# Planned costs of the Fourier sets, and the order of the products in K's table sets

## The chip, the cores and the metric

One core of a Trainium2 chip runs the kernel. The metric is device time in microseconds (us): the median of several executions. The core's engines each work through a list of instructions in order: TensorE (PE) multiplies matrices into PSUM; VectorE (DVE), ScalarE (ACT) and GpSimd (POOL) do elementwise work; SyncE (SP), POOL and ACT start DMA transfers.

## The reference

The output mixes two layers of one input, u (2048 tokens by 512 channels), with a gate per token. a is a state space layer: a kernel K(d, l) of 2048 taps for each channel, convolved with u by FFTs of length 4096, plus a skip term. b is a gated linear unit on x.

```python
def _A_ref(u, log_A_real, A_imag, C_real, C_imag, log_dt, D_skip):
    dt = jnp.exp(log_dt)
    A = -jnp.exp(log_A_real) + 1j * A_imag
    C = (C_real + 1j * C_imag) * dt[:, None]
    P = jnp.exp((A * dt[:, None])[:, :, None] * pos[None, None, :])
    K = 2.0 * jnp.einsum("dn,dnl->dl", C, P).real
    Kf, Uf = jnp.fft.rfft(K, 2 * L), jnp.fft.rfft(u_t, 2 * L)
    y = jnp.fft.irfft(Uf * Kf[None, :, :], 2 * L)[:, :, :L]
    return y.transpose(0, 2, 1) + u * D_skip[None, None, :]

def _B_ref(x, w_gate, w_up, w_down):
    h = jnp.einsum("bsd,df->bsf", x, w_gate) * jnp.einsum("bsd,df->bsf", x, w_up)
    return jnp.einsum("bsf,fd->bsd", h, w_down)

g = _sigmoid((x * gate_w).sum(-1, keepdims=True))
return g * a + (1 - g) * b
```

## The kernel before, in words

The GLU (b) fills PE from beginning to end. Its 14 tiles of hidden features are taken in four groups, and within a group four chunks of 512 tokens are gone through. Each float32 factor is split into a high and a low part, so that one product becomes three matmuls of 128 by 128 by 512 ("whi", "wlo", "hh", "hl", "dhi", "dlo" are such parts). `product` (line 580) issues three for the gate or up projection into `pg` or `pu`, `down` (line 623) three for the down projection into `y`. Between them ACT and DVE make h = gate times up and its two parts, `hh` and `hl`.

The state space layer (a) is put between the GLU's matmuls as *sets*: each set is one task of PE, a run of small float32 matmuls that use the array split into tiles. Each float32 product stands in the trace as two weight loads and two matmuls. The sets, all writing PSUM banks called `k`:

- `u_part`, `first` (line 731 on): the first transform of u, 8 sets, tiles of 32 rows by 64 columns.
- `k_block`, `kgen` (lines 1081 and 1084): the **table set**, 16 of them, one for each block of 32 channels. DVE and ACT build two tables of powers, x and v, for the block; PE multiplies them, for each channel d one product with the real parts (c = 0) and one with the imaginary parts (c = 1), which accumulate in one place. A product has 128 rows, 32 columns of weights and 64 moving columns, and goes to the column tile d % 4 of the array, which is also the quarter of the bank's partitions that it writes. After the set ACT and DVE fold the bank `pk` into `kt`.
- `k_first` (line 1112): K's first transform, 8 sets on four tiles of 32 rows by 128 columns.
- `m_second` (line 1197): second transforms of u and K, 16 sets, tiles of 32 by 32.
- `m_inverse` (line 1254): after the product of the spectra, the first inverse transform, 8 sets, tiles of 32 rows by 64 columns.
- `m_last` (line 1304): the last inverse transform, 5 sets, tiles of 64 by 32; one for two groups of rows or for one.

The order of the work is not written by hand. Every piece is a task, given to `add` with its engine, a cost in us, its operands, a rank and the tiles that it holds. `Work.run` (line 301) is a list scheduler: it keeps a clock for each engine, works out when each task could start (operands ready, buffer free, engine free), and takes the task with the earliest start; rank decides between equals. Sets that carry `many` are kept at least 6 us (4 us in the last parts) from the end of the one before. The list that comes out is each engine's order of instructions, for the DMA queues too. On the chip only that order counts: an instruction starts when its operands are there and its engine has done what stands before it. The costs given to `add` therefore never cost time themselves; they only shape the order.

All instructions pass through one helper, so every row of the profile names line 124; rows are told apart by the names of their tiles.

Of the kernel before, what the change touches and what calls it, by code (L numbers as in the profile page):

```python
# [20 lines left out]
KT = D // P  # L21
# [343 lines left out]
def gated_mix_kernel(  # L365
# [365 lines left out]
    def u_part(t):  # L731
        ut = inp([P, 4, D])
        rs = slice(4 * t, 4 * t + 4)
        add("sp", 0.42, lambda: sp.dma_start(ut.t, uv[:, rs, :]), w=[ut], dma=1024, after=6.0 + (U_STEP + 1.0) * t)

        def score_of(j):
            r = 4 * t + j
            pr = new("mid", "y", [P, D], bufs=2)
            add(
                "dve", 0.73,  # L740
                lambda: dve.scalar_tensor_tensor(
                    pr.t, ut.t[:, j, :], 1.0, gw.t, op0=ALU.mult, op1=ALU.mult, accum_out=gate[:, r : r + 1]
                ),
                r=[ut, gw], w=[pr, (m_gate, ("s", t))], rank=0,
            )

        for j in range(4):
            score_of(j)
        ones = [new("mid", "y", [P, 2, D], bufs=2) for _ in range(2)]
        ops = (ALU.add, ALU.subtract)  # L750
        for y, op in zip(ones, ops):
            add(
                "dve", 1.22,
                lambda y=y, op=op: dve.tensor_tensor(out=y.t, in0=ut.t[:, :2], in1=ut.t[:, 2:], op=op), r=[ut], w=[y],
            )
        for s, op in enumerate(ops):
            for d, y in enumerate(ones):
                add(
                    "dve", 0.69,
                    lambda d=d, s=s, y=y, op=op: dve.tensor_tensor(  # L760
                        out=ut.t[:, 2 * s + d], in0=y.t[:, 0], in1=y.t[:, 1], op=op
                    ),
                    r=[y], w=[(ut, 2 * s + d)],
                )

        def first(s):
            banks, st = [bank() for _ in range(4)], new("mid", "ev", [P, KT, 4, P], bufs=2)

            def fn():
                for p in range(2):  # L770
                    col, src = 64 * (p + s), 2 * s + (p + s) % 2
                    for tq in range(4):
                        lanes = slice(32 * tq, 32 * tq + 32)
                        pe.matmul(
                            banks[tq].t[64 * p : 64 * p + 64], w1_t.t[lanes, col : col + 64], ut.t[lanes, src],
                            start=True, stop=True, tile_position=(32 * tq, 64 * p),
                        )

            add("pe", 1.3, fn, r=[(ut, 2 * s), (ut, 2 * s + 1), w1_t], w=banks, rank=1, hold=[st])
            for tq in range(4):  # L780
                add(
                    "act", 0.59,
                    lambda tq=tq: act.copy(st.t[:, :, tq], banks[tq].t.rearrange("p (f d) -> p f d", f=KT)),
                    r=[banks[tq]], w=[(st, tq)],
                )
            n0 = 16 * s + 4 * t
            for q in range(KT):
                add(
                    "pool", 0.95,
                    lambda q=q: pool_q.dma_start(  # L790
                        su_d[q, :, n0 : n0 + 4, :], st.t[:, q],
                    ),
                    r=[st], w=[(m_su, (q, n0))], dma=256,
                )

        for s in range(2):
            first(s)
        sc, ga = (m_gate, ("s", t)), (m_gate, t)
        add("act", 1.5, lambda: act.activation(gate[:, rs], gate[:, rs], AF.Tanh, scale=0.5), r=[sc], w=[sc], rank=0)

        def gates():
            dve.tensor_scalar(ngate[:, rs], gate[:, rs], -0.5, 0.5, op0=ALU.mult, op1=ALU.add)
            dve.tensor_scalar(gate[:, rs], gate[:, rs], 0.5, 0.5, op0=ALU.mult, op1=ALU.add)

        add("dve", 0.4, gates, r=[sc], w=[ga, sc], rank=0)
# [272 lines left out]
    def apart_of(q):  # L1078
        return work.LESS if q >= KT - 2 else work.APART

    def k_block(b, x, v):
        pk = bank()

        def kgen():
            pv = pk.t.rearrange("p (g j) -> p g j", j=64)
            for d in range(TB):
                ch, g = d % 4, d // 4
                for c in range(2):
                    pe.matmul(
                        pv[32 * ch : 32 * ch + 32, g, :], x.t[:, c, d, :], v.t[:, c, d, :], start=c == 0, stop=c == 1,  # L1090
                        tile_position=(0, 32 * ch),
                    )

        if b % 4 == 0:
            kts["now"] = new("tab", "kt", [P, 2, 2, 32, 16])
        kt, g0 = kts["now"], b % 4 * 8
        add("pe", 2.15, kgen, r=[x, v], w=[pk], rank=0, hold=[kt], many=work.APART, slack=5.0 if b < 16 else 0.0)
        pv = lambda a: pk.t.rearrange("p (g a b k) -> p g a b k", a=2, b=2, k=16)[:, :, a]
        side = lambda h: kt.t[:, h, :, g0 : g0 + 8].rearrange("p b g k -> p g b k")
        add("act", 0.37, lambda: act.copy(side(1), pv(0)[:, :, :, ::-1]), r=[pk], w=[(kt, (1, b % 4))])  # L1100
        for h, op in enumerate((ALU.add, ALU.subtract)):
            add(
                "dve", 0.42, lambda h=h, op=op: dve.tensor_tensor(out=side(h), in0=pv(1), in1=side(1), op=op),
                r=[pk, (kt, (1, b % 4))], w=[(kt, (h, b % 4))], rank=0,
            )
        if b % 4 == 3:
            k_first(b // 4, kt)
# [4 lines left out]
    def k_first(q, kt):  # L1112

        tt(
            0.24, lambda: kt.t[:, :, 0, :, 0], lambda: kt.t[:, :, 0, :, 0],
            lambda: skip[:, q].unsqueeze(1).broadcast_to([P, 2, 32]), ALU.add, [m_skip], [kt],
        )
        for h in range(2):
            banks = [bank() for _ in range(4)]
            if q < KT - 1:  # L1120
                st = new("mid", "ev", [P, 16, 4, 32], bufs=2)
                sts = [(0, 16, st)]
            else:
                shape = [P, 8, 4, 32]
                pair = [new("tab", n, shape) for n in ("ri", "e")] if h else [stage(shape) for _ in range(2)]
                sts = [(0, 8, pair[0]), (8, 8, pair[1])]

            def fn(h=h, banks=banks):
                for b in range(2):
                    for c in range(4):  # L1130
                        lanes = slice(32 * c, 32 * c + 32)
                        pe.matmul(
                            banks[c].t, w1k_t[lanes, b, 64 * h : 64 * h + P],
                            kt.t[lanes, h, b].rearrange("p g k -> p (g k)"),
                            start=b == 0, stop=b == 1, tile_position=(32 * c, 0),
                        )

            add("pe", 1.95, fn, r=[kt, m_w1k], w=banks, rank=-1, hold=[st for _, _, st in sts], many=apart_of(q))
            for n0, n, st in sts:
                for c in range(4):  # L1140
                    ns = slice(n0, n0 + n)
                    evict(
                        q, c, 0.2 + 0.025 * n, lambda c=c, st=st: st.t[:, :, c, :],
                        lambda c=c, banks=banks, ns=ns: banks[c].t.rearrange("p (g n) -> p n g", n=16)[:, ns],
                        [banks[c]], [(st, c)],
                    )
                n0 += 16 * h
                add(
                    "sp", 0.42,
                    lambda n0=n0, n=n, st=st: sp.dma_start(  # L1150
                        sk_d[q, :, n0 : n0 + n, :], st.t.rearrange("p n c g -> p n (c g)"),
                    ),
                    r=[st], w=[(m_sk, (q, m)) for m in range(n0, n0 + n, 8)], dma=64 * n,
                )
# [42 lines left out]
    def m_second(q, T, ins, w):  # L1197
# [13 lines left out]
                to = banks[r].t[32 * c : 32 * c + 32].rearrange("l (p d) -> l p d", p=2)[:, p]  # L1211
                pe.matmul(to, w.t[lanes, m], src[lanes, c, p], start=True, stop=True, tile_position=(32 * r, 32 * c))

        add("pe", 1.05, fn, r=[*parts, w], w=banks, rank=1, hold=[to])
        for r in range(4):
            h, e = divmod(r, 2)
            evict(
# [36 lines left out]
    def m_inverse(q, T0, ys, ws):  # L1254
# [18 lines left out]
                                    ys[t].t[lanes, k, e, cs], start=k == 0, stop=k == 1, tile_position=(32 * j, 64 * e),  # L1273
                                )

        add("pe", 2.13, fn, r=[*ys, *ws], w=[*banks, (m_turn, (q, T0))], rank=1, hold=sts, many=apart_of(q), slack=0.0 if q < KT - 1 else 0.0)
        for j in range(4):
            st, m = sts[j // 2], j % 2
            evict(
# [24 lines left out]
    def m_last(q, gs):  # L1304
# [14 lines left out]
        def fn():  # L1319
# [8 lines left out]
                        )  # L1328

        add(  # L1330
            "pe", 0.2 + 0.86 * len(gs), fn, r=[*src, m_w4, *([(m_turn, (KT - 1, 2))] if q == KT - 2 else [])], w=[b for bs in banks for b in bs], rank=1,
            hold=[to for _, to, _, _ in pieces],
        )
        cs = slice(P * q, P * q + P)
# [155 lines left out]
```

## Time and profile before

| what | value |
|---|---|
| median of 3 runs | 588.23 us (587.84 to 588.41) |
| span of the profiled execution, first to last instruction | 586.6 us |
| outside the span (median less span) | 1.6 us |
| DMA traffic | 136.28 MB, mean 232 GB/s |

The page gives no device time of the profiled execution itself beside its span, so the median of the runs stands for it; the 1.6 us are before the first and behind the last instruction. In rows of the timeline the first number is the start and the second the time until the last of the merged instructions ends; matmuls are pipelined, so one of them starts long before the one before it has ended, and it is the distance between starts that counts. In a row of groups, "k<-v,x 128*32 128x64 f32 x2048" is a tile written from two others, the rows and columns of the array in use, the moving operand, and the count. "PEld" is the loading of weights.

### The profile page before, as it was taken

Reading aid. Unit: us, or ns where it says so; the run is one execution under the profiler, and the core shown is the slowest. Engines: PE = TensorE matmul, PEld = TensorE weight load, DVE = VectorE, ACT = ScalarE, POOL = GpSimd, SP = SyncE. Lnnn points to the kernel's source line nnn. Section 1 sums busy time; section 2 is a strip of 40 time slices with the busy share of each in tenths; the row PEclk is TensorE's granted clock in tenths of the full one; section 3 lists DMA queues with packets and bytes.
Section 4 is the critical chain, followed back from the end, with each engine's and each line's share of the span. In section 5 each row is a group of like instructions: output and inputs, shape, how many; then the busy total and the mean of one; then the engine's idle time right before and its main releaser. Section 6 shows DMA issues by size and latency. Waiting matters only on the chain.

```text
span 586.6 us, 14827 instructions
## 1 busy us (share of the span) xinstructions
PE 576.4 (98%) x5996; PEld 433.9 (74%) x5996; DVE 511.3 (87%) x812; ACT 399.0 (68%) x891; POOL 113.4 (19%) x159
## 2 busy tenths in 40 slices
PE   8999999999989999999999999999999999999997
PEld 5777777877876777887777778777878787677775
DVE  6998999999999999999799999995999982367664
ACT  5468888898578589876968764899696523443351
POOL 0002222311102231310412200421321104011011
PEclk9999999999999999999999999999999999999999
DMA  8999969997647698998697859899958349899976
GB/s 276 383 369 357 374 241 319 289 257 212 125 154 181 194 272 205 228 245 297 135 257 249 183 180 304 158 187 276 221 136 212 65 143 230 290 270 253 283 159 125
DMA packets 71687, 136.28 MB, mean 232 GB/s; under 512 B 6852, under 2 KB 35780, under 8 KB 69188
## 3 DMA queue, kind: packets, MB, share of 16 engines
q1 hardware_dynamic: 47668, 87.10, 43.0%
q0 software_dynamic: 23392, 47.98, 39.5%
q8 instruction: 47, 0.77, 0.6%
q10 hardware_dynamic: 560, 0.26, 0.2%
q14 instruction: 20, 0.16, 0.1%
HBM read 80.27 MB, written 55.05 MB: 231 GB/s over the span
## 4 chain that ended last, share of the span: by engine, by line
PE 83%; DVE 6%; ACT 4%; DMA 4%; issue 1%; SPq 0%; DVEq 0%; ACTq 0%
PE pg L124 23%; PE pu L124 23%; PE y L124 22%; PE k L124 16%; DVE v L124 1%; DMA pb<-par_d 1%; DMA xs_d<-xs 1%; DVE x L124 1%; DMA y<-in_xT 1%; DMA xs<-xs_d 1%; ACT acc L124 1%; DVE t L124 1%; ACT ev L124 1%; ACT xs L124 1%; ACT e L124 1%
## 5 line engine op out<-in xcount | busy, mean ns | idle before, releaser
L124 PE MATMUL pg<-xs,whi 128*128 128x512 f32 x448 | 138.9, 391 | 1.0 <-DVE xs L124 0.6
L124 PE MATMUL pu<-xs,whi 128*128 128x512 f32 x448 | 138.3, 390 | 0.0
L124 PEld LDWEIGHTS pg<-xs,whi 128*128 128x128 f32 x448 | 84.2, 188 | 20.2 <-ACT whi L124 2.0
L124 PEld LDWEIGHTS pu<-xs,whi 128*128 128x128 f32 x448 | 84.2, 188 | 16.9
L124 PE MATMUL y<-dhi,hl 128*128 128x512 f32 x224 | 90.3, 403 | 2.9 <-DVE hl L124 2.4
L124 PE MATMUL pu<-xs,wlo 128*128 128x512 f32 x224 | 90.1, 402 | 0.0
L124 PE MATMUL pg<-xs,wlo 128*128 128x512 f32 x224 | 89.4, 399 | 0.4 <-ACT h L124 0.4
L124 PE MATMUL y<-dlo,hh 128*128 128x512 f32 x224 | 87.5, 391 | 0.0
L124 PE MATMUL y<-dhi,hh 128*128 128x512 f32 x224 | 87.3, 390 | 0.0
L124 POOL DMA_DIRECT2D out<-acc x44 | 40.2, 968 | 180.4 <-ACT acc L124 173.0
L124 ACT COPY ev<-k 128x512 f32<-128x512 f32 x112 | 58.8, 596 | 14.5 <-PE k L124 14.4
L124 ACT CAST hh<-h 128x512 fp32r<-128x512 f32 x56 | 34.6, 618 | 45.7 <-DVE h L124 45.5
L124 PEld LDWEIGHTS y<-dhi,hl 128*128 128x128 f32 x224 | 42.0, 187 | 24.4 <-issue 8.1
L124 DVE TENSOR_TENSOR h<-pu,h 128x512 f32<-128x512 f32 x56 | 38.5, 688 | 23.6 <-PE pu L124 23.0
L124 PEld LDWEIGHTS pu<-xs,wlo 128*128 128x128 f32 x224 | 42.0, 187 | 20.0 <-issue 10.7
L124 ACT ACTIVATE acc<-y,ngate 128x512 f32<-128x512 f32 x62 | 41.7, 685 | 21.9 <-PE y L124 18.9
L124 PEld LDWEIGHTS pg<-xs,wlo 128*128 128x128 f32 x224 | 42.1, 188 | 18.4 <-issue 6.9
L124 ACT COPY h<-pg 128x512 f32<-128x512 f32 x56 | 32.9, 587 | 28.3 <-PE pg L124 22.0
L124 PEld LDWEIGHTS y<-dhi,hh 128*128 128x128 f32 x224 | 42.1, 188 | 9.1
L124 PEld LDWEIGHTS y<-dlo,hh 128*128 128x128 f32 x224 | 42.1, 188 | 8.2 <-DVE dlo L124 0.3
L124 DVE TENSOR_TENSOR hl<-h,hh 128x512 fp32r<-128x512 f32 x56 | 38.4, 686 | 3.0 <-ACT hh L124 2.7
L124 PEld LDWEIGHTS k<-v,x 128*32 128x32 f32 x2048 | 30.6, 109 | 6.4 <-issue 4.7
(130 smaller groups left out, 965.4 us busy)
## 6 DMA issues: line engine op xcount, KB each, us to landing
xs<-xs_d SPq DMA_DIRECT2D x36, 512.0 KB, 5.8
out<-acc POOLq DMA_DIRECT2D x44, 256.0 KB, 5.9
raw<-in_wts SPq DMA_DIRECT2D x33, 256.0 KB, 5.6
xs_d<-xs SPq DMA_DIRECT2D x16, 512.0 KB, 6.6
su_d<-ev POOLq DMA_DIRECT2D x32, 256.0 KB, 6.3
y_d<-ts SPq DMA_DIRECT2D x28, 256.0 KB, 4.9
in<-su_d POOLq DMA_DIRECT2D x12, 512.0 KB, 5.9
sk_d<-ev SPq DMA_DIRECT2D x6, 1024.0 KB, 5.4
```

The source lines that it names most:

```text
L124: got = getattr(self.engine, name)(*args, **kw)
```

## The change

Six costs of sets change: u's first transform 1.3 to 1.245, the table set 2.15 to 2.05, K's first transform 1.95 to 2.13, the second transform 1.05 to 1.27, the inverse 2.13 to 2.225, the last 0.2 to 0.36 beside its 0.86 for each group of rows. And `kgen` issues the same 64 products in another order: before, channel by channel, both products of a channel behind each other on one column tile; after, for each four channels first the four products with c = 0, one on each column tile, then the four with c = 1.

```diff
-            add("pe", 1.3, fn, r=[(ut, 2 * s), (ut, 2 * s + 1), w1_t], w=banks, rank=1, hold=[st])
+            add("pe", 1.245, fn, r=[(ut, 2 * s), (ut, 2 * s + 1), w1_t], w=banks, rank=1, hold=[st])
...
         def kgen():
             pv = pk.t.rearrange("p (g j) -> p g j", j=64)
-            for d in range(TB):
-                ch, g = d % 4, d // 4
+            for g in range(TB // 4):
                 for c in range(2):
-                    pe.matmul(
-                        pv[32 * ch : 32 * ch + 32, g, :], x.t[:, c, d, :], v.t[:, c, d, :], start=c == 0, stop=c == 1,
-                        tile_position=(0, 32 * ch),
-                    )
+                    for ch in range(4):
+                        d = 4 * g + ch
+                        pe.matmul(
+                            pv[32 * ch : 32 * ch + 32, g, :], x.t[:, c, d, :], v.t[:, c, d, :], start=c == 0, stop=c == 1,
+                            tile_position=(0, 32 * ch),
+                        )
...
-        add("pe", 2.15, kgen, r=[x, v], w=[pk], rank=0, hold=[kt], many=work.APART, slack=5.0 if b < 16 else 0.0)
+        add("pe", 2.05, kgen, r=[x, v], w=[pk], rank=0, hold=[kt], many=work.APART, slack=5.0 if b < 16 else 0.0)
...
-            add("pe", 1.95, fn, r=[kt, m_w1k], w=banks, rank=-1, hold=[st for _, _, st in sts], many=apart_of(q))
+            add("pe", 2.13, fn, r=[kt, m_w1k], w=banks, rank=-1, hold=[st for _, _, st in sts], many=apart_of(q))
...
-        add("pe", 1.05, fn, r=[*parts, w], w=banks, rank=1, hold=[to])
+        add("pe", 1.27, fn, r=[*parts, w], w=banks, rank=1, hold=[to])
...
-        add("pe", 2.13, fn, r=[*ys, *ws], w=[*banks, (m_turn, (q, T0))], rank=1, hold=sts, many=apart_of(q), slack=0.0 if q < KT - 1 else 0.0)
+        add("pe", 2.225, fn, r=[*ys, *ws], w=[*banks, (m_turn, (q, T0))], rank=1, hold=sts, many=apart_of(q), slack=0.0 if q < KT - 1 else 0.0)
...
-            "pe", 0.2 + 0.86 * len(gs), fn, r=[*src, m_w4, *([(m_turn, (KT - 1, 2))] if q == KT - 2 else [])], w=[b for bs in banks for b in bs], rank=1,
+            "pe", 0.36 + 0.86 * len(gs), fn, r=[*src, m_w4, *([(m_turn, (KT - 1, 2))] if q == KT - 2 else [])], w=[b for bs in banks for b in bs], rank=1,
```

## The prediction

> **What bounds the kernel now.** I read the page first, then the table by stages, then PE's timeline around the sets that the change touches. On the page, look at PE's share and at the chain that ended last:
>
> ```profile
> span 586.6 us, 14827 instructions
> PE 576.4 (98%) x5996; PEld 433.9 (74%) x5996; DVE 511.3 (87%) x812; ACT 399.0 (68%) x891; POOL 113.4 (19%) x159
> PE 83%; DVE 6%; ACT 4%; DMA 4%; issue 1%; SPq 0%; DVEq 0%; ACTq 0%
> ```
>
> An average of 98% may hide stages, so here are stages (the columns are length, PE, PEld, DVE, ACT, POOL busy, clock, DMA share, GB/s):
>
> ```profile
> 60.00:100.00 40.00, 39.56 (x227) 27.94 (x226) 39.86 (x72) 33.32 (x77) 10.58 (x20) 1.00 0.85 307
> 100.00:140.00 40.00, 39.86 (x412) 32.51 (x411) 38.91 (x57) 37.60 (x84) 10.25 (x14) 1.00 0.90 246
> 140.00:176.00 36.00, 33.63 (x384) 27.01 (x382) 35.59 (x57) 23.63 (x59) 3.41 (x4) 1.00 0.62 173
> 176.00:240.00 64.00, 64.00 (x759) 47.28 (x758) 62.07 (x90) 51.70 (x111) 14.04 (x16) 1.00 0.83 212
> ...
> 420.00:480.00 60.00, 60.00 (x584) 47.10 (x583) 58.39 (x89) 37.26 (x88) 8.77 (x10) 1.00 0.55 142
> 480.00:540.00 60.00, 59.37 (x855) 43.04 (x854) 29.99 (x49) 22.46 (x45) 12.45 (x14) 1.00 0.92 264
> ```
>
> From 176 us on PE has no idle time but 0.63 us after 480; what is taken off its list there comes off the end. From 60 to 176 us DVE is as full (39.86 of 40 us), and PE waits for it now and then. The largest such wait:
>
> ```profile
> 171.66 0.61 PE L124 MATMUL pg<-xs,whi 128*128 128x512 f32 x2
> 173.91 0.50 PE L124 MATMUL y<-dhi,hl 128*128 128x512 f32 x1 [1.63 <-DVE hl L124]
> ```
>
> After PE's last matmul start only some 4 us are left (586.6 − 582.46), which the change doesn't touch:
>
> ```profile
> 582.46 0.39 PE L124 MATMUL y<-dhi,hh 128*128 128x512 f32 x1
> ```
>
> **The change, part by part.** No instruction is added or removed. Two things differ: the order of the 64 products in each of K's 16 table sets, and six costs that the list scheduler plans with.
>
> *What a set costs.* PE's timeline around a table set, an inverse set, a first transform of K, a second transform and a last one:
>
> ```profile
> 251.86 0.61 PE L124 MATMUL pg<-xs,whi 128*128 128x512 f32 x2
> 252.41 2.07 PE L124 MATMUL k<-v,x 128*32 128x64 f32 x128
> 254.40 0.50 PE L124 MATMUL pg<-xs,wlo 128*128 128x512 f32 x1
> 254.74 0.62 PE L124 MATMUL pg<-xs,whi 128*128 128x512 f32 x2
> ```
> ```profile
> 243.50 0.39 PE L124 MATMUL y<-dlo,hh 128*128 128x512 f32 x1
> 243.72 0.39 PE L124 MATMUL y<-dhi,hh 128*128 128x512 f32 x1
> 244.04 2.09 PE L124 MATMUL k<-y,w3s 32*64 32x128 f32 x128
> 246.07 0.50 PE L124 MATMUL y<-dhi,hl 128*128 128x512 f32 x1
> 246.40 0.40 PE L124 MATMUL y<-dlo,hh 128*128 128x512 f32 x1
> ```
> ```profile
> 176.17 2.00 PE L124 MATMUL k<-kt,w1k_t 32*128 32x512 f32 x16
> 178.10 0.50 PE L124 MATMUL y<-dhi,hl 128*128 128x512 f32 x1
> ```
> ```profile
> 206.45 1.14 PE L124 MATMUL k<-in,w2s 32*32 32x512 f32 x32
> 207.52 0.50 PE L124 MATMUL y<-dhi,hl 128*128 128x512 f32 x1
> ```
> ```profile
> 276.58 1.95 PE L124 MATMUL k<-in,w_t 64*32 64x512 f32 x32
> 278.46 0.50 PE L124 MATMUL y<-dhi,hl 128*128 128x512 f32 x1
> ```
>
> Matmuls of the GLU start 0.23 us apart (243.50, 243.72). Into a set the step is 0.32 (243.72 to 244.04), and after it one step is 0.33 or 0.34 (246.07 to 246.40; 254.40 to 254.74): a change of tile mode costs 0.09 + 0.11 = 0.20 us beside the set. The table set itself takes 254.40 − 252.41 = 1.99, with the changes 2.19; the inverse 2.03 and 2.23; K's first transform 1.93 and 2.13; the second 1.07 and 1.27; the last 1.88 and 2.08. The planner's new costs for the last four are 2.225, 2.13, 1.27 and 0.36 + 2 × 0.86 = 2.08: what the trace has. The table set's is 2.05, 0.14 below the trace. So that one figure claims a shorter set; the others only describe.
>
> *What the new order can save in a set.* Medians of the records (min/median/max ns):
>
> ```profile
> L124 PEld LDWEIGHTS k<-v,x x2048: 106/110/110, 101.2 to 493.2; 128*32 128x32 f32 x187
> L124 PE MATMUL k<-v,x x2048: 216/219/243, 101.2 to 493.2; 128*32 128x64 f32 x187
> L124 PE MATMUL k<-kt,w1k_t x128: 587/587/692, 176.2 to 505.3; 32*128 32x512 f32 x128
> ```
>
> From 64 to 512 columns a record grows by 587 − 219 = 368 ns, 0.82 ns a column. Streaming alone is then, for the busiest tile: table set, 128 records on four column tiles, 32 × 64 × 0.82 = 1.68 us; inverse, 128 on eight, 16 × 128 × 0.82 = 1.68; K's first, 16 on four, 4 × 512 × 0.82 = 1.68; second, 32 on sixteen, 0.84; last, 32 on eight, 1.68. What is left over (filling, draining, tiles that wait for each other) is 0.31 in the table set, 0.35 in the inverse, 0.25 in K's first, 0.23 in the second, 0.20 in the last. So the four column tiles run side by side already, and the order can win back only a part of 0.31. Bounds: if the table set's rest becomes that of the last transform, it gains 0.11; if it becomes that of the inverse, which has as many records and already goes from tile to tile, it loses 0.04. K's first transform, which like the table set has four tiles split along one side, gives 0.06. I take 0.08, between 0.06 and 0.11, since the diff's own figure (0.14, a rest that no set here shows) pulls upward; all of it, −0.04 to 0.14, stays in the range.
>
> The table set's loads last 110 ns, and 128 of them end to end would be 14.1 us; the set takes 1.99, so they overlap with matmuls of the set. [...]
>
> *The sum.* Sixteen table sets; the first four (starts up to 167 us) lie where DVE is full, so I count them half: what PE gains there may return as a longer wait for hl. The other twelve lie where PE is never idle. 14 × 0.08 = 1.1 us. The evacuations of pk wait for the whole set as before and come 0.08 earlier; nothing else is hidden or uncovered, because the GLU's matmuls follow at once.
>
> *The plan.* K's first transform is planned 0.18 longer (8 sets), the second 0.22 (16), the inverse 0.095 (8), the last 0.16 (5), u's first 0.055 shorter (8), the table set 0.10 shorter (16): in the plan PE's list grows by 1.4 + 3.5 + 0.8 + 0.8 − 0.4 − 1.6 = 4.5 us, on the chip by nothing. Every queue's order can shift: which GLU products stand between sets, which DVE and ACT pieces go first, and SP's and POOL's transfers behind them. From 176 to 540 us PE waited for no engine, with an order planned on sets 0.1 to 0.2 too short; planned right, the other engines get no later due times. I cost this at nothing there. The cover is that PE always has a GLU product ready; if it is gone, one wait costs about what the largest does now, 1.63. Another unknown is a hole inside a set, "issue", that no engine explains:
>
> ```profile
> 490.39 1.97 PE L124 MATMUL k<-v,x 128*32 128x64 f32 x117
> 493.00 0.43 PE L124 MATMUL k<-v,x 128*32 128x64 f32 x11 [0.63 <-issue]
> 493.36 0.50 PE L124 MATMUL y<-dhi,hl 128*128 128x512 f32 x1
> ```
>
> This set takes 2.97 instead of 1.99, so a hole costs 0.98. With another spacing of the sets it may go or another may come; I count it as staying, with ±1.0 in the range.
>
> The span is 586.6, the median 588.2 (1.6 more lies around the span). 588.2 − 1.1 = **587.1 us**.
>
> **Rivals.** 0.2% of this time, 1.2 us, is about what a measurement of this kernel can tell from no change.
>
> *The set shrinks as far as the diff says.* For it: the other new costs equal the trace to 0.01, so 2.05 may be read from one too. Against: no set shows a rest as low as 0.17. 16 × 0.14 = 2.2, so 586.0; with the hole gone as well, 585.0.
>
> *The order of the products changes nothing in the set.* The table of PE's records of the set by stages of 0.224 us counts the records that touch each stage:
>
> ```profile
> 252.70:252.93 0.22, 0.22 (x31) 1.00 1.09 210
> 252.93:253.15 0.22, 0.22 (x31) 1.00 0.73 155
> 253.15:253.38 0.22, 0.22 (x32) 1.00 1.19 238
> 253.82:254.05 0.22, 0.22 (x31) 1.00 1.21 265
> ```
>
> The count is level from 0.3 us into the set on: the old order doesn't starve one column tile while another works. Only filling and draining could then be shortened, by 0 to 0.04 a set: 587.5 to 588.2, no change. [...]
>
> *The new list makes PE wait in the stretch where DVE is full.* Place: 60 to 176 us, where PE now loses 0.44, 0.14 and 2.37 us (row lengths less PE). If the shifted planned times let a piece of a table (DVE) go ahead of h or hl, PE waits as at 171.66, 1.63 each time. One more gives 587.1 + 1.6 = 588.7; two give 590.3, slower by 0.4%. It decides from 2.3 us of new waits (1.1 + 1.2). For it: DVE has no room there, and a list order jumps at small shifts. Against: only u's and the table sets stand there, and their costs move by 0.1 or less.
>
> **How the numbers follow.** Forecast (0.06 to 0.11 a set, the plan neutral, 586.5 to 587.4): 0.40, its shorter half faster, the rest the same. The diff's figure: 0.23, faster. Nothing in the set: 0.19, nearly all the same. New waits: 0.18, slower but for 0.02. Faster 0.20 + 0.23 + 0.01 = 0.44; slower 0.16; the same 0.40. The range goes from 585.0 (the diff's figure and the hole gone) to 589.6 (between one and two new waits).
>
> **What would show it.** Table set: from its start to the GLU's next 1.91 (1.99 − 0.08) in all sixteen; 1.85 speaks for the first rival, 1.95 or more for the second. Plan: PE busy 64.00 of 64 and 60.00 of 60 from 176 us on, waits for hl before 176 summing to about what they do now, one hole of 1 us by "issue" and not three. Wrong would be: a set shorter by 0.08 while the end doesn't move (then another wait took its place), or an end that moves by over 2.5 us with sets as they were (then the list order made it).

## The result, and the profile after

The changed kernel takes 594.11 us (median of 5, 592.96 to 594.70), the kernel before beside it 588.23 (587.84 to 589.71): a ratio of 1.0097, 95% interval 1.0083 to 1.0110. The forecast was 587.1, with a range up to 589.6. The time went up by 5.9 us where 1.1 less was forecast. One of the 17 runs of the kernel before that stand beside the first group of experiments was slow (671.15 us at a granted clock of 0.805) and is left out everywhere.

The page of the changed kernel first: span, engines, and the shares of the chain that ended last.

```profile
span 592.6 us, 14826 instructions
PE 579.0 (98%) x5996; PEld 434.8 (73%) x5996; DVE 511.0 (86%) x812; ACT 398.7 (67%) x891; POOL 113.5 (19%) x159
PE 77%; DVE 11%; ACT 6%; DMA 3%; issue 2%; DVEq 0%; ACTq 0%
```

The span is 6.0 longer (586.6 before). PE's share of the span is still 98%, so the page alone hides where the time went. The stages (length, PE, PEld, DVE, ACT, POOL busy, clock, DMA share, GB/s) show it:

```profile
140.00:176.00 36.00, 34.47 (x388) 27.86 (x387) 35.63 (x57) 24.42 (x61) 3.71 (x5) 1.00 0.66 176
176.00:240.00 64.00, 61.61 (x741) 44.90 (x740) 58.38 (x84) 48.26 (x105) 14.24 (x16) 0.97 0.80 204
240.00:300.00 60.00, 59.58 (x653) 45.10 (x653) 56.05 (x89) 49.37 (x113) 15.39 (x16) 1.00 0.96 236
300.00:360.00 60.00, 58.74 (x838) 44.76 (x838) 57.93 (x84) 41.98 (x96) 9.71 (x11) 1.00 0.75 203
360.00:420.00 60.00, 59.38 (x653) 45.42 (x652) 53.28 (x79) 49.54 (x112) 16.54 (x17) 1.00 0.94 226
```

The last three of these stages in the kernel before:

```profile
240.00:300.00 60.00, 60.00 (x657) 45.94 (x656) 56.06 (x87) 50.16 (x115) 14.74 (x16) 1.00 0.94 237
300.00:360.00 60.00, 60.00 (x933) 45.33 (x934) 57.27 (x84) 39.08 (x89) 10.61 (x11) 1.00 0.80 211
360.00:420.00 60.00, 60.00 (x580) 46.06 (x569) 52.88 (x78) 50.61 (x115) 16.61 (x18) 1.00 0.95 223
```

From 176 to 420 us, where the forecast wanted 64.00 of 64 and 60.00 of 60, PE now idles in every stage: 2.39 us in the first, 1.26 in the third. From 420 to 540 us it is full. From 140 to 176 us it lost less than before (34.47 busy against 33.63). What PE waited for, the first three rows of its waits over the whole span (us in total, times, longest):

```profile
PE k L124 <- issue: 4.3, 3, 2.4
PE pg L124 <- ACT h L124: 1.6, 2, 1.2
PE y L124 <- DVE hl L124: 1.5, 2, 1.4
```

For the kernel before, the same answer has, among others:

```profile
PE y L124 <- DVE hl L124: 2.4, 2, 1.6
PE k L124 <- issue: 0.6, 1, 0.6
```

The wait that grew is "issue" inside sets: 0.6 us once, now 4.3 in three. PE's timeline of the changed kernel shows an undisturbed table set, then those three holes:

```profile
256.89 1.99 PE L124 MATMUL k<-v,x 128*32 128x64 f32 x128
258.81 0.50 PE L124 MATMUL pg<-xs,wlo 128*128 128x512 f32 x1
...
208.91 1.14 PE L124 MATMUL k<-in,w2s 32*32 32x512 f32 x32
209.98 0.50 PE L124 MATMUL y<-dhi,hl 128*128 128x512 f32 x1
...
211.24 0.39 PE L124 MATMUL y<-dhi,hh 128*128 128x512 f32 x1
211.56 1.97 PE L124 MATMUL k<-v,x 128*32 128x64 f32 x122
215.93 0.43 PE L124 MATMUL k<-v,x 128*32 128x64 f32 x6 [2.39 <-issue]
216.29 0.80 PE L124 MATMUL y<-dhi,hl 128*128 128x512 f32 x1
216.88 0.63 PE L124 MATMUL y<-dlo,hh 128*128 128x512 f32 x1
217.31 0.63 PE L124 MATMUL y<-dhi,hh 128*128 128x512 f32 x1
...
335.28 2.06 PE L124 MATMUL k<-y,w3s 32*64 32x128 f32 x124
338.61 0.43 PE L124 MATMUL k<-y,w3s 32*64 32x128 f32 x4 [1.26 <-issue]
338.97 0.50 PE L124 MATMUL pg<-xs,wlo 128*128 128x512 f32 x1
...
417.37 1.98 PE L124 MATMUL k<-v,x 128*32 128x64 f32 x124
419.97 0.31 PE L124 MATMUL k<-v,x 128*32 128x64 f32 x4 [0.62 <-issue]
420.21 0.50 PE L124 MATMUL y<-dhi,hl 128*128 128x512 f32 x1
```

The undisturbed set takes 258.81 − 256.89 = 1.92 (1.99 before). The set at 211.56 takes 216.29 − 211.56 = 4.73, so its hole costs 2.81; the inverse at 335.28 takes 3.69 instead of 2.03 (1.66), the table set at 417.37 takes 2.84 (0.92). All three stop with 4 to 6 matmuls to go, and those read tiles of the same names as the matmuls ahead of the stop. After the first one the GLU's matmuls start 0.43 apart (216.88, 217.31) instead of 0.23; the stage there says why:

```profile
216.00:219.00 3.00, 3.00 (x12) 2.27 (x12) 2.19 (x4) 2.59 (x12) 0.00 (x0) 0.50 0.83 189
```

The granted clock is 0.50 for these 3 us, right after a hole of 2.4 us, which costs another 1.4. In the kernel before, the table set that follows the same second transform (206.45) comes after 27 matmuls of the GLU and runs through:

```profile
213.54 0.39 PE L124 MATMUL y<-dhi,hh 128*128 128x512 f32 x1
213.86 2.07 PE L124 MATMUL k<-v,x 128*32 128x64 f32 x128
215.86 0.50 PE L124 MATMUL y<-dhi,hl 128*128 128x512 f32 x1
```

In the changed list only 6 stand between them. The account of the 6.0 us: table sets 16 × −0.072 (1.996 before, 1.924 now, in the sets without a hole) = −1.15; time lost inside sets 1.92 before and 7.05 now, +5.1; the low clock +1.4. The rest, about +0.6, has no place in this account: the waits for other engines in PE's list add up to 5.6 before and 5.5 now. Of the 7.05, the three holes above are 5.39; a second transform at 434.75 is 1.05 longer, where two of its loads wait for ACT's evictions (0.36 us at 435.31, 0.35 at 435.80), and two small ones make 0.6. Of the 1.92 before, 0.97 is the hole at 490.39 and 0.95 a second transform at 329.48, whose loads stop at 330.

**What the holes have in common.** The page has a DMA queue for instructions (packets, MB, share):

```profile
q8 instruction: 47, 0.77, 0.5%
```

0.77 MB in 47 packets is 16.4 KB each; PE's 2 × 5996 loads and matmuls and some 100 waits are 12,100 instructions, so about 256 a packet if the queue is PE's, which I take it to be from these counts. I numbered PE's records from 0 by their starts (loads, matmuls, and the 100 or so waits and drains between them) and set the holes beside the packets' own records in the trace. This table is worked out from those records and is no view of the profile:

| kernel, hole (us) | record at the hole | mod 256 | last packet landed | PE resumes after that |
|---|---|---|---|---|
| before, 492.15 to 493.00 | 10177 | 193 | 491.63 | 1.37 |
| after, 213.32 to 215.93 | 3521 | 193 | 214.62 | 1.31 |
| after, 337.07 to 338.61 | 6593 | 193 | 337.34 | 1.27 |
| after, 419.13 to 419.97 | 8385 | 193 | 418.68 | 1.29 |

All four holes lie a multiple of 256 records apart, at the same remainder, and end 1.3 to 1.4 us after a packet has landed. The loads of the second transform at 329.48 stop at such a place too (record 6337, again 193, going on 1.68 after a packet). That is how it would look if PE had run out of instructions at an *edge*, the place between two packets; the experiments test it. The GLU uses 24 instructions in 2.72 us, so a packet lasts it 29 us; a table or an inverse set is 256 instructions in 1.9 or 2.0 us. The 256 of the counts and the 256 between the holes agree.

### The profile page after: what moved, and what is told of

Same layout as the page of the kernel before. It is cut to its first block, busy times and chain, and to the rows that moved or that the text cites. A ratio compares the mean times of both kernels' runs of the same rounds, so it can differ in the third digit from the quotient of the medians.

```text
span 592.6 us, 14826 instructions
## 1 busy us (share of the span) xinstructions
PE 579.0 (98%) x5996; PEld 434.8 (73%) x5996; DVE 511.0 (86%) x812; ACT 398.7 (67%) x891; POOL 113.5 (19%) x159
## 4 chain that ended last, share of the span: by engine, by line
PE 77%; DVE 11%; ACT 6%; DMA 3%; issue 2%; DVEq 0%; ACTq 0%
PE y L124 22%; PE pg L124 21%; PE pu L124 20%; PE k L124 14%; DMA raw<-in_wts 3%; DVE v L124 2%; DVE x L124 2%; DVE h L124 1%; DVE hl L124 1%; DVE y L124 1%; DVE t L124 1%; ACT v L124 1%; DMA y<-in_xT 1%; ACT e L124 1%; ACT ev L124 1%
```

## The experiments

Theories. **F** (fetch): the new list lets packets of 256 instructions run out faster than the next one lands; what decides is where the sets lie against the edges of the packets. **W** (waits): the new list makes PE wait for other engines, and "issue" is only how some of that is shown. Apart from both stands the question whether the order of the products or the list made the loss. The runs came in two groups, each on one chip; the kernel before took 588.52 us in the first (16 runs), 587.93 in the second (29). Each ratio goes by the runs of its own group.

**The new order of the products alone.** Only the change in `kgen`; all six costs as before, so the list is the old one.

> The products of the table set in turn, every planned cost as before, so that the list is that of before. Theory F (holes in PE's own instruction stream make the loss; the new order of products is a gain): sixteen sets 0.07 us shorter (1.92 to the next GLU matmul in place of 2.00), the two holes of before at the same instructions, 588.2 - 1.1 = 587.1 us. Rival W (the list order makes engines wait for each other; the products' order is beside the point) says the same here. Rival O (the shorter set itself starves something): 590 us or more.

Measured: 587.28 (12 runs), 0.998 of before (0.9965 to 0.9995). A table set in its timeline:

```profile
253.56 1.99 PE L124 MATMUL k<-v,x 128*32 128x64 f32 x128
255.49 0.50 PE L124 MATMUL pg<-xs,wlo 128*128 128x512 f32 x1
```

255.49 − 253.56 = 1.93. In time the order gains about what was forecast (0.05 to 0.35%), and this kernel is the fastest of the three. One expectation missed: the list and its edges are those of before, but only one of the two holes of before came again, the second transform at 330 us (record 6337, 0.81 lost). At record 10177 the packet had landed 2.7 us before PE came to the edge, and there is no hole. So this edge made a hole only where its packet was late (in the trace of before PE went on 1.37 us after it), and that differed between these two executions.

**The new costs alone.** The six cost lines, `kgen` as before.

> The six new planned costs, the products of the table set in the old order: the list is that of the changed kernel. Theory F and rival W: the whole loss comes with the list, 594.1 + 1.1 = 595.2 us, holes at the same instructions as in the changed kernel. Rival O: about 588.

Measured: 594.5 (6 runs), 1.011 (1.0089 to 1.0131). The sets that lose time are the same (212, 335, 415, 433 us), two of them at records 3521 and 8385 again, ending 1.44 and 1.58 after a packet landed; the inverse at 335 loses only 0.35 here. The hole at record 3521 is larger than in the changed kernel (2.85 by "issue"), yet the granted clock behind it stays at 1.00, so the low clock does not follow every such hole. The whole loss is the list's.

**The kernel before, its instructions shifted by 176.** At the start of the program PE runs two products into a scratch bank (`warm`); one of them gives way to 45 small ones. The list is not touched, nor is any set; each later instruction only lies 176 places further on against the packets.

```diff
-            for _ in range(2):
-                pe.matmul(scratch.t, zero.t[:, :P], zero.t, start=True, stop=True)
+            for n in range(45):
+                c = n % 4
+                pe.matmul(
+                    scratch.t[32 * c : 32 * c + 32, :8], zero.t[:32, :32], zero.t[:32, :8], start=True, stop=True,
+                    tile_position=(0, 32 * c),
+                )
+            for _ in range(1):
+                pe.matmul(scratch.t, zero.t[:, :P], zero.t, start=True, stop=True)
```

> The kernel before, its list unchanged, with 176 more PE instructions ahead of the first GLU matmul (45 products of 32 by 32 by 8 in place of one of the two warming products of 128 by 128 by 512), which PE issues while it waits for its first data. Theory F: PE's instructions come in packets of 256; 176 more in front move every packet's edge by 176 instructions, and from the sets' places in the trace of before the edges then fall where sets stand close together: holes sum to about 6.5 us in place of 2.4, so 588.2 + 4.1 = 592.3 us, with no other wait added. Rival W: the list is the same, so the time is the same, 588.2 within 0.5.

Measured: 591.35 (6 runs), 1.0055 (1.0037 to 1.0073). A hole has come where the list before had none:

```profile
219.47 1.08 PE L124 MATMUL k<-in,w2s 32*32 32x512 f32 x15
221.78 1.09 PE L124 MATMUL k<-in,w2s 32*32 32x512 f32 x17 [1.23 <-issue]
```

It is at record 3777, 193 mod 256, and ends 1.24 after a packet landed; the set takes 2.26 longer by it. W gives no reason for it, since no task and no set has changed. A second one, at 558 us (record 11969), costs 0.59, and both holes of before are gone, as their records are no longer at an edge. The sizes missed: 2.85 is lost inside sets where about 6.5 was expected, against 1.92 before. Much of the rest of this trace's extra time is its start: the first matmuls of the GLU lie 0.43 apart until 11 us, which costs 2.0 against the trace of before. In the trace of the new order alone, without any small product, the same costs 1.5, so it differs between executions without any shift.

**The kernel before, shifted by a whole packet** (the same edit with 65 small products, 256 instructions). This is the control for the 176: more extra work, but every set lies as before against the edges.

> Control to the shift by 176: the kernel before, its list unchanged, with 256 more PE instructions in front (65 small products in place of one warming product). That is one whole packet, so every packet's edge falls on the same instruction of the list as before. Theory F: holes as in the kernel before (about 2 us), 588.5 us, up to 1.0 more for the longer start; clearly under the 591.35 of the shift by 176. Rival P (the small products in front do the harm themselves, by a cold start or later loads): 591.35 or more, since there are more of them.

Measured: 588.38 (12 runs), 1.0024 (1.0007 to 1.0040). The same second transform is whole, 221.34 − 220.27 = 1.07:

```profile
220.27 1.14 PE L124 MATMUL k<-in,w2s 32*32 32x512 f32 x32
221.34 0.50 PE L124 MATMUL pu<-xs,wlo 128*128 128x512 f32 x1
```

The second transform that had lost 0.95 in the kernel before stops again, at record 6593 = 6337 + 256, and loses 0.70; the hole of 490 is missing, as with the new order alone. So the holes go by the edges and not by the added work. The time says it less plainly: the medians are 0.45 apart for 256 instructions and 2.8 for 176, but by the ratios the control too is slower than the kernel before, by 0.24% against 0.55%, and the two intervals touch.

**The changed kernel, shifted by 104** (27 small products), to move the set at 211 off its edge.

> The changed kernel with 104 more PE instructions in front (27 small products in place of one warming product), its list unchanged. Theory F: the edges of the instruction packets move away from the places where sets stand close; holes sum to about 2.5 us in place of 6.0, and the stretch of slow clock after the largest hole (216 to 219 us) goes: 594.1 - 3.5 - 1.5 = 589 us, at most 590.6. Rival W: 594.1 within 0.5.

Measured: 592.8 (6 runs), 1.0083 (1.0061 to 1.0104); a miss. The three holes of the changed kernel and the low clock are gone; two others came, at 279.8 (0.52) and 328.5 (1.43). (The second transform at 433.5 loses 0.89, much as the one at 434.75 did.) The hole at 328.5 stands between matmuls of the GLU, in no set at all:

```profile
328.50 0.40 PE L124 MATMUL y<-dlo,hh 128*128 128x512 f32 x1
330.15 0.50 PE L124 MATMUL y<-dhi,hh 128*128 128x512 f32 x1 [1.25 <-issue]
```

It is at record 6337, 193 mod 256 again, 1.47 after a packet. So a stop by "issue" is not tied to the small matmuls of the sets. The holes thus did what F expected: they fell from 5.39 to 1.95 us, with the 1.4 of the low clock on top. The time did not follow: in the same trace the start was 1.1 longer, and the waits for other engines rose from 5.5 to 8.8, among them 1.5 for h behind the set at 127.7 us. Why they rose with an unchanged list, no run shows. Against the changed kernel's own 1.0097 the intervals overlap, so this shift has not been shown to mend the time.

**The changed kernel, shifted by a whole packet** (65 small products).

> The changed kernel, its list unchanged, with 256 more PE instructions in front: the edges fall on the same instructions as in the changed kernel. Theory F: the holes of the changed kernel are back at the same sets (the table set at 211 us, the inverse at 335, the table set at 417, the second transform at 434), 594 to 595.5 us, above the 592.8 of the shift by 104. Rival W: no difference between the two shifts, 592.8 within 0.5.

Measured: 593.57 (6 runs), 1.0099 (1.0074 to 1.0125). The holes are back in the three sets of the changed kernel (starting at 212, 335 and 419 us), at records 256 further on (3777, 6849, 8641); a fourth (record 9153) costs 0.95 in the table set at 440, and the second transform at 437 loses only 0.28, where 434 had been expected to be back. The largest:

```profile
212.34 1.97 PE L124 MATMUL k<-v,x 128*32 128x64 f32 x122
216.94 0.43 PE L124 MATMUL k<-v,x 128*32 128x64 f32 x6 [2.62 <-issue]
```

It stops after the same 122 matmuls. The time is a little under the forecast's lower end, and its interval overlaps that of the shift by 104, so time alone doesn't tell the two shifts apart; the places of the holes do. The profile fell on the slowest of the six (596.38), with the low clock behind two holes, of 2.62 and 1.70 us by "issue".

**Second transforms kept apart in the list.** Unlike the table sets, K's first transforms and the inverses, they carry no `many`, so the scheduler may set one close ahead of a table set, as at 208.91. The changed kernel with one argument more; a second transform then starts at least 2.5 us after the end of the set before it, in the plan, and the next set with `many` keeps its 6 us to it.

```diff
-        add("pe", 1.27, fn, r=[*parts, w], w=banks, rank=1, hold=[to])
+        add("pe", 1.27, fn, r=[*parts, w], w=banks, rank=1, hold=[to], many=2.5)
```

> The changed kernel with one more planned rule: the second transforms too are kept apart from the other dense sets (2.5 us behind the one before, and the one after 6 us behind them). Theory F: no two dense sets follow each other within one packet's time, holes fall from about 7 to about 2 us and the stretch of slow clock goes; with the shorter table sets 586 to 588 us, below the kernel before. Rival W: a list with the same costs, 594 within 2, with holes or waits as in the changed kernel.

Measured: 587.91 (12 runs), 1.0007 (0.9988 to 1.0026), so no different from the kernel before (it had been expected below it), and 0.9% below the changed one (1.0097). Page and stages of its profiled execution (586.15, among the fastest of the twelve):

```profile
span 584.4 us, 14838 instructions
...
176.00:240.00 64.00, 64.00 (x759) 47.15 (x758) 60.94 (x88) 50.81 (x110) 15.07 (x17) 1.00 0.80 207
300.00:360.00 60.00, 60.00 (x844) 45.66 (x843) 57.57 (x87) 43.55 (x107) 14.13 (x14) 1.00 0.77 197
360.00:420.00 60.00, 60.00 (x683) 45.05 (x682) 56.47 (x81) 52.02 (x118) 12.97 (x14) 1.00 0.93 245
```

PE is full again in the stages that had lost 2.39, 1.26 and 0.62, and inside sets 0.40 us is lost instead of 7.05. Two stops remain between matmuls of the GLU, at 263.8 and 488.4 us (records 4801 and 10177, 193 mod 256), about 0.5 each.

**A second list of this kind**, to see whether that was one lucky list: `many=3.0`, and the table set planned at 2.12.

> As the run before, but the second transforms 3.0 us behind the one before, and the table set planned with 2.12, the cost that the trace of the changed kernel shows: another list by the same rule. Theory F: again about 2 us of holes, 586 to 588.5 us. If the gain of the run before were a lucky list, this one would lie anywhere between 586 and 594.

Measured: 589.51 (12 runs), 1.0013 (0.9991 to 1.0035); the median is 1.0 above the forecast's upper end, the ratio no different from 1. Inside sets 0.56 us is lost, and one stop between matmuls of the GLU is left (record 4801). Two such lists of two have hardly a hole in their traces; since each is another list, their sets lie otherwise against the edges too.

**Closer sets, or the place of the edges?** The traces can be counted for this. Take PE's records from 60 us on, without the stops, and let the edges fall at each of the 256 possible places in turn: how many packets would be used up in under 4 us? On average over the places 3.7 in the list of before, 3.9 in the changed one, 3.6 in each of the two kept apart. At the place where the edges did fall, 193, it is 3, 8, 5 and 2. By this count the changed list is no more crowded than the old one, and keeping the second transforms apart hardly thins it; its edges fell at a bad place, where the count over all places goes from 0 to 9.

What stays open: why the twelve executions of these two kernels (the profiled ones took 586.15 and 586.99) spread over some 5.8 us, the kernel before over 5.2 in the same group; which of the six costs moved the sets to the edges; and whether the load on the DMA engines decides how late a packet is. After the first 60 us of the traces of before and after, a packet landed between 3.2 us ahead of PE's coming to the edge before its own and 6.5 us behind it; a packet of 256 instructions was used up in under 4 us three times in the kernel before and eight times in the changed one, and not each time made a hole.

## Why the prediction was wrong

**The table set: right.** 0.08 was forecast, 0.072 measured, and alone it gave 587.28 where 587.1 stood. Of the order's rivals neither held: 1.92 is neither 1.85 nor 1.95. The bound that it was taken from, what the other sets lose beside streaming (an estimate from the 0.82 ns a column of the records), served well; what inside the set the order shortens, be it filling, draining or tiles that wait for each other, no run shows. The level count of records in the set was no argument that the order is without effect, and the 0.072 is more than the 0.04 that this rival allowed.

**The plan: the failed step.** "I cost this at nothing there", with the cover "that PE always has a GLU product ready". PE did have one ready; what it lacked, going by the stops at the edges, was the instruction. It was not enough here, as the description of the kernel before has it, that operands were there and the engine was done with what stood before: at the three stops in the sets of the changed kernel PE went on 1.27 to 1.31 us after a packet of instructions had landed. The second half of the step saw the place, a hole inside a set that "may go or another may come", but counted it "as staying, with ±1.0 in the range". I took it for an accident of one set and didn't ask what made it. It was the one row of the trace of before with the cause in it: 117 of 128 matmuls, then a stop that no engine explains. The same page counts 47 instruction packets, from which about 256 a packet follows, against 256 instructions in one set. The term measured +5.1 inside sets (of it 5.39 against 1.92 in stops at edges) and +1.4 by the clock behind the largest hole, where ±1.0 stood. By the count above it was bad luck that the edges of this list fell as they did, and six costs don't tell it; but that such stops can come and go with any new list was to be read from the trace, and the range left it out.

**New waits for DVE, the rival on the slow side: right sign, wrong mechanism and place.** It stood for 60 to 176 us and for hl; hl cost 1.5 instead of 2.4, and PE's busy time from 60 to 176 us hardly moved (113.05 us before, 113.24 now). What came was after 176, where the list stood at nothing.

**The tests named** told it apart as meant: "an end that moves by over 2.5 us with sets as they were (then the list order made it)" holds but for the 0.07 a set, and of "one hole of 1 us by 'issue' and not three" it was three.

**How far the cause is shown.** That the list makes the loss: shown, by the two halves of the change each alone. That the holes are PE waiting for its instructions: the stops sit at 193 mod 256 in every trace that has any; they move with a shift by 176 or 104 and stay on the same instructions with one by 256; and over all ten traces, with 463 edges, PE never went past an edge sooner than 1.24 us after its packet had landed, while the stops end 1.2 to 1.7 us after it. What makes the 193 and the 1.2 us isn't shown. That crowding in the new list, and not where the edges happened to fall, made so many holes: not shown; the count over all places of the edges speaks for the place, and the two lists kept apart have other places too. About 1.05 of the loss, the second transform at 434.75, stands at no edge.

## What to carry to other kernels

A planned cost that equals the trace better doesn't make a better list: judge a scheduler's new list by how it lies on the chip, and change costs and code one at a time, since here the code alone gains 0.2% and the costs alone lose 1.1%. Where a burst of small matmuls holds as many instructions as one instruction packet (here 256 in 1.9 or 2.0 us, where the GLU by its 24 in 2.72 us would take 29), suspect a late packet behind a stop by "issue": number the records and see whether the stops share a remainder. A shift of all instructions, as here, tells whether the stops hang on the edges or on the list. A small row that no engine explains is worth its cause before its size goes into a range.

## What the runs showed of the hardware

47 packets of 16.4 KB landed in the instruction queue for PE's 12,100 instructions, about 256 a packet, and the stops lay multiples of 256 records apart. PE stopped at such an edge inside sets (2.39 us by "issue" at 215.93 in the changed kernel) and between matmuls of the GLU (1.25 us at 330.15 in the shift by 104), and went on 1.2 to 1.7 us after the packet had landed; the stops inside the sets named were up to 3.1 us long between starts, and the packet used up ahead of the three in the changed kernel had lasted 3.3, 3.0 and 3.0 us. After the stop at 213.32 of 2.6 us between starts, the granted clock was 0.50 for about 3 us; after one of 3.1 us in the run with the new costs alone it stayed at 1.00. And the order in which products go to the four column tiles was worth 0.07 of 1.99 us, although with the old order the count of records at work was already level, 31 or 32 a stage of 0.224 us from 0.3 to 1.6 us into the set.
